# A gated MLP's second down projection: three pairs of weight-sum loads and ScalarE's transposing loads change places

## The chip, the cores and the metric

The kernel runs on one core of a Trainium2 chip. The metric is the device time of one execution in microseconds; the median of three runs counts. A profile of one execution shows what each engine did: PE (matrix multiply; PEld is its weight load), DVE (vector), ACT (scalar), POOL (GpSimd) and SP, which here only starts transfers. A q behind the name (SPq, ACTq) is the engine's queue of instructions that start transfers or wait.

## The reference

```python
x: (1, 2048, 1024) bf16;  w_gate, w_up: (1024, 3584);  w_down: (3584, 1024)
g = einsum("bsd,df->bsf", x, w_gate)
u = einsum("bsd,df->bsf", x, w_up)
h = gelu(g, tanh form) * u
out = einsum("bsf,fd->bsd", h, w_down)
```

## The kernel before

The 2048 rows of x are taken in two passes of 1024, each in two halves of 512 columns of the transposed x. A pass makes h (gate, up, gelu, product) and then runs its down projection. All large products are made with seven block products in place of eight, so sums and differences of blocks stand in for the blocks themselves; those of w_down are made once, in the first pass, written to a buffer in DRAM (`td`) and loaded again by each down projection. "Stored weight sums" are these.

The change is in the second down projection, `down(..., last=True)`, the last 103 us of the span (PE's first matmul of it starts at 436.82). It goes through numbered steps, mostly four or eight matmuls of 128x512 each. `step()` is called ahead of each group of matmuls and carries out what an agenda lists for that step: `at(last, step, what, ...)` fills it, from tables of step numbers. Within a step and between steps each engine's instructions stand in the order of the program text. The index j runs over 14 pairs of blocks of h and w_down.

- `load12(j)` loads the stored sums of pair j, two tiles q of 128x512 fp32 (L642; for some j as one larger tile m, L636, or w, L631). `LAST12[j]` is its step.
- `make12(j)` makes two sums of h on DVE (step `LAST12S[j]`).
- `fetch73(j)` loads raw blocks of w_down (L662, step `RAW73[j]`); `make73(j)`, step `LAST73[j]`, makes from them and from h three tiles on DVE and one cast on ACT (L677 for j under 8, L133 from 8).
- `apart`, steps 31 to 50, is one of the seven block products, itself split in the same way into products called K1, K2, K22, K3 and K4 (four steps each). Its results are split into 16-bit planes on ACT (L733) and written to DRAM by SP (`pt`, L734).
- `turn_back(quad, n)` loads these planes with a transposing transfer (L745): the eight of quad 0 from ACT's queue, the eight of quad 1 from SP's. `put_0` and `join_1` put them together on ACT (L750) and add them to what DVE stores; `put_0` also needs a tile of earlier sums (`ud`), loaded by SP at L757.

PE runs two loops. In the first one (steps 28 to 30 ahead of `apart`, 51 to 65 behind it) e(t) is four matmuls with the second tile of `load12(t)`, and c(t), which stands four steps later, four with the first; e(11) is the first to need a pair that the change moves. In the second one (steps 66 to 79) e(t) and c(t) use the tiles of `make73(t)`; c(6) to c(13) come last. Ahead of the second loop's e(0) ACT copies the four result banks of the first loop out (L138).

Every transfer ends by raising one of eight semaphores. The program deals these out in turn, in text order and over both queues together, and a transfer is not started until the previous one on its semaphore has landed. A queue starts its transfers in order, so a transfer that waits holds all those behind it.

Of the kernel before, what the change touches and what calls it, by code (L numbers as in the profile page):

```python
# [10 lines left out]
def kernel(  # L11
# [60 lines left out]
    D2 = 2 * P  # L72
    ORD4 = [*range(0, NJ, 2), *range(1, NJ, 2)]
    MSTEPS = 17
    LAST12 = [14, 15, 16, 29, 30, None, None, 41, 41, None, None, 49, 50, 51]
    LAST12S = [16, 18, 20, 34, 37, 40, 43, 45, 47, 49, 51, 53, 55, 57]
    BIG12L = (5, 9)
    RAW73 = [40, 40, 40, 40, 51, 51, 52, 53, 54, 55, 56, 57, 59, 59]
    LAST73 = [52, 53, 55, 57, 59, 61, 63, 65, 66, 68, 70, 71, 72, 73]
    LATE3 = 6  # L80

# [724 lines left out]
    def at(last, step, what, *args):  # L806
        agenda.setdefault((last, int(step)), []).append((what, args))

    for last in (False, True):
# [6 lines left out]
        for j in range(NJ):  # L816
            if (LAST12 if last else AT12)[j] is not None:
                at(last, (LAST12 if last else AT12)[j], load12, j, last)
            at(last, (LAST12S if last else AT12S)[j], make12, j, last)
            at(last, RAW73[j] if last else AT73[j] - 3, fetch73, j)  # L820
            at(last, (LAST73 if last else AT73)[j], make73, j, last)
# [7 lines left out]
    for i in range(NI):  # L829
        at(1, 2 * i, make_si, i)  # L830
    for n in range(2 * NS):
        at(1, 52 + n // 2, turn_back, 0, n)
        at(1, 63 + n, turn_back, 1, n)
    for i in range(NS):
        at(1, 69 + i, put_0, i)
# [488 lines left out]
```

## Time and profile before

| | us |
|---|---|
| median of 3 runs (541.85 to 543.47) | 542.02 |
| the profiled execution | 542.01 |
| its span, first to last instruction | 540.2 |
| PE busy in the span | 530.9 (98%) |
| DVE / ACT / POOL busy | 404.5 / 302.1 / 268.3 |
| mean granted TensorE clock | 0.994 |

The profiled execution is 1.8 us longer than its span; that part is taken as fixed. In the views below a line of the timeline gives the start, the length, the engine, the line of the program, the operation, tile written<-tiles read, shapes and the count, and in brackets the idle time before it with what ended it. Matmuls overlap, so a group's length is longer than its share: the next group's start tells the pace.

### The profile page before, as it was taken

How to read it: one execution, taken by the hardware profiler on the slowest of the kernel's cores; microseconds unless marked ns; L12 is line 12 of the kernel's file. 1: busy time of each engine (PE TensorE's matmuls, PEld its weight loads, DVE VectorE, ACT ScalarE, POOL GpSimd, SP SyncE). 2: the span in 40 equal slices, each digit the busy share in tenths (PEclk: the TensorE clock that was granted, in tenths of full speed). 3: DMA queues.
4: the chain of work that ended last, by engine and by line, in shares of the span. 5: the costliest groups of instructions: out<-in, count | busy, mean ns of one | idle time of the engine just before them, and what ended most of it. 6: DMA issues, size and time to landing. Idle time of an engine off the chain costs nothing.

```text
span 540.2 us, 7756 instructions
## 1 busy us (share of the span) xinstructions
PE 530.9 (98%) x2375; PEld 376.4 (70%) x2375; DVE 404.5 (75%) x645; ACT 302.1 (56%) x544; POOL 268.3 (50%) x259
## 2 busy tenths in 40 slices
PE   9999999999999999999999999999999999998797
PEld 5568686868686764688867586766866754776685
DVE  2989768787777786659699877657668598796875
ACT  3557686968686831016577775565666621371480
POOL 1079968979797950000005989796897500000000
PEclk9999999999999999999999999999999999999799
DMA  9795227685767799999997999928344798698943
GB/s 247 170 245 157 78 76 275 198 291 195 233 235 243 246 373 388 350 317 234 242 292 221 294 317 344 260 75 228 111 132 116 270 354 281 226 315 203 287 100 117
DMA packets 140729, 126.09 MB, mean 233 GB/s; under 512 B 31632, under 2 KB 119184, under 8 KB 140560
## 3 DMA queue, kind: packets, MB, share of 16 engines
q1 hardware_dynamic: 136336, 124.55, 75.4%
q10 hardware_dynamic: 4352, 1.05, 0.9%
q8 instruction: 19, 0.31, 0.2%
q14 instruction: 22, 0.18, 0.1%
HBM read 86.38 MB, written 31.06 MB: 217 GB/s over the span
## 4 chain that ended last, share of the span: by engine, by line
PE 93%; DMA 2%; DVE 2%; ACTq 1%; ACT 1%; issue 0%; SPq 0%; DVEq 0%
PE bank L145 92%; ACTq L745 1%; DMA q<-td 1%; DVE q L121 1%; PE bank L1057 1%; DMA w<-pt 1%; DVE xT L121 1%; PE bank L1002 1%; ACT s L875 0%; ACT xT L733 0%; ACT u L138 0%; DVE st L121 0%; ACT xT L677 0%; SPq L642 0%; ACTq L733 0%
## 5 line engine op out<-in xcount | busy, mean ns | idle before, releaser
L124 POOL TENSOR_TENSOR s<-w 128x512 fp32r<-128x512 bf16 x102 | 117.5, 1170 | 48.1 <-DMA w<-in_w_gate_dram 33.7
L145 PE MATMUL bank<-t,s 128*128 128x512 f32 x528 | 126.3, 392 | 0.0
L145 PEld LDWEIGHTS bank<-t,s 128*128 128x128 f32 x528 | 99.0, 188 | 21.6 <-POOL s L124 0.3
L145 PE MATMUL bank<-xT,w 128*128 128x512 bf16 (+1 forms) x504 | 110.2, 376 | 0.0
L145 PEld LDWEIGHTS <-w 128*128 128x128 bf16 x504 | 47.9, 98 | 57.9 <-issue 4.2
L213 ACT ACTIVATE g<-sum 128x512 f32<-128x512 f32 x81 | 51.5, 636 | 60.2 <-DVE sum L121 57.9
L138 ACT COPY p<-bank 128x512 f32<-128x512 f32 x98 | 55.1, 590 | 46.9 <-PE bank L145 46.8
L145 PE MATMUL bank<-q 128*128 128x512 f32 x224 | 57.5, 397 | 5.2 <-DMA q<-td 4.2
L121 DVE TENSOR_TENSOR hT<-g,bank 128x512 bf16<-128x512 f32 x72 | 49.0, 687 | 17.5 <-ACT g L213 12.1
L124 POOL TENSOR_TENSOR s<-w,s 128x512 fp32r<-128x512 bf16 x50 | 57.8, 1174 | 0.4
L124 POOL TENSOR_TENSOR s<-s,w 128x512 fp32r<-128x512 f32 x50 | 57.4, 1167 | 0.2
L121 DVE TENSOR_TENSOR bank<-bank,p 128x512 f32<-128x512 f32 x74 | 51.3, 695 | 5.9 <-PE bank L145 5.3
L145 PE MATMUL bank<-t,sa 128*128 128x512 f32 x216 | 54.9, 397 | 0.0
L145 PE MATMUL bank<-tb,s 128*128 128x512 f32 x216 | 54.3, 393 | 0.0
L199 POOL COPY seen<-t 128x1 f32<-128x1 f32 x2 | 0.4, 184 | 106.7 <-DVE t L121 106.7
L145 PEld LDWEIGHTS bank<-q 128*128 128x128 f32 x224 | 42.4, 190 | 15.6 <-DVE q L121 6.0
L145 PEld LDWEIGHTS bank<-t,sa 128*128 128x128 f32 x216 | 40.6, 188 | 9.1
L145 PEld LDWEIGHTS bank<-tb,s 128*128 128x128 f32 x216 | 40.5, 188 | 9.0 <-POOL s L124 0.3
L121 DVE TENSOR_TENSOR sum<-bank,p 128x512 f32<-128x512 f32 x54 | 37.0, 686 | 12.3 <-PE bank L145 11.3
L138 ACT COPY u<-bank 128x512 f32<-128x512 f32 x62 | 35.5, 596 | 17.5 <-PE bank L145 14.1
L133 ACT CAST tb<-raw 128x512 fp32r<-128x512 bf16 x20 | 12.5, 632 | 37.1 <-PE bank L145 24.2
L133 ACT CAST sa<-w 128x512 fp32r<-128x512 bf16 x54 | 30.7, 617 | 2.9 <-DMA out_dram<-st 2.9
(121 smaller groups left out, 736.8 us busy)
## 6 DMA issues: line engine op xcount, KB each, us to landing
raw<-in_w_down_dram SPq DMA_DIRECT2D x72, 256.0 KB, 5.5
w<-in_w_gate_dram SPq DMA_DIRECT2D x27, 512.0 KB, 4.5
w<-in_w_up_dram SPq DMA_DIRECT2D x27, 512.0 KB, 6.0
td<-m SPq DMA_DIRECT2D x11, 768.0 KB, 4.6
q<-td SPq DMA_DIRECT2D x28, 256.0 KB, 5.3
pd<-xT SPq DMA_DIRECT2D x10, 512.0 KB, 5.7
w<-td SPq DMA_DIRECT2D x5, 1024.0 KB, 7.8
p<-pd SPq DMA_DIRECT2D x20, 256.0 KB, 4.9
```

Source lines behind the costliest of these rows:

```text
L121: nc.vector.tensor_tensor(out=out, in0=a, in1=b, op=op)
L124: nc.gpsimd.tensor_tensor(out=out, in0=a, in1=b, op=op)
L133: nc.scalar.copy(out=t, in_=src)
L138: nc.scalar.copy(out=t, in_=ps)
L145: nc.tensor.matmul(ps, lhsT=lhs, rhs=rhs, start=start, stop=stop, skip_group_check=True)
L199: nc.gpsimd.tensor_copy(out=seen, in_=tile[:, :1].bitcast(f32))
L213: nc.scalar.activation(g, src, ACT.Gelu_apprx_tanh)
L745: queue.dma_start_transpose(out=turned["tp", quad][:, i, half], in_=pt[2 * quad + half][:, i * P : (i + 1) * P])
L1002: nc.tensor.transpose(tp[:, ko, :], xn[i][:, ko * P : (ko + 1) * P], ident)
L1057: nc.tensor.matmul(bank[3][:, :cols], lhsT=warm[:, :P], rhs=warm[:, :cols], start=True, stop=True)
```

## The change

Only step numbers change. `load12` of pairs 11, 12 and 13 moves from steps 49, 50, 51 to 40, 41, 49. `fetch73` of pairs 2 and 3 moves from step 40 to 48 and 49, and that of pair 4 from 51 to 50. The eight transposing loads of quad 0, which ACT starts, move from steps 52 to 55 to steps 56 to 59. No instruction is added or removed, and no size changes.

```diff
-    LAST12 = [14, 15, 16, 29, 30, None, None, 41, 41, None, None, 49, 50, 51]
+    LAST12 = [14, 15, 16, 29, 30, None, None, 41, 41, None, None, 40, 41, 49]
...
-    RAW73 = [40, 40, 40, 40, 51, 51, 52, 53, 54, 55, 56, 57, 59, 59]
+    RAW73 = [40, 40, 48, 49, 50, 51, 52, 53, 54, 55, 56, 57, 59, 59]
...
     for n in range(2 * NS):
-        at(1, 52 + n // 2, turn_back, 0, n)
+        at(1, 56 + n // 2, turn_back, 0, n)
         at(1, 63 + n, turn_back, 1, n)
```

In SP's order the two loads of pair 11 now stand behind the raw blocks of pairs 0 and 1, those of pair 12 behind the two m loads of pairs 7 and 8, those of pair 13 behind the first four plane writes; before, pairs 11 and 12 stood behind these four writes and pair 13 behind the last two writes and two raw loads. On ACT the first transposing load now stands behind the casts of pairs 0, 1 and 2; before, behind that of pair 0.

## The prediction

> **What bounds the kernel now.** I read the page's chain first, then the chain in order of time, then who waited for whom, then PE's timeline of the last stage, then that of the two queues.
>
> PE carries 93% of the chain, so only time in which PE waits, or runs slowly, can be won. The chain has one long piece that isn't PE's, and it ends in the load of a stored pair:
>
> ```profile
> 496.87 6.19 DMA q<-td
> 503.06 0.14 issue
> 503.19 33.69 PE bank L145 x136
> 536.88 0.02 issue
> 536.91 0.69 DVE st L121
> ```
>
> The waits (us in total, times, longest) name that load, a shorter wait of PE for DVE, and, of SP's queue, what held the loads:
>
> ```profile
> PE bank L145 <- DMA q<-td: 4.2, 1, 4.2
> PE bank L145 <- DVE q L121: 0.9, 1, 0.9
> SPq L642 <- DMA w<-pt: 4.6, 1, 4.6
> ```
>
> A stored-sum load (q) stood 4.6 us in SP's queue until a transposing load (w<-pt), started by ACT, had landed: the shared semaphores. PE's timeline shows the cost:
>
> ```profile
> 494.85 1.07 PE L145 MATMUL bank<-m,q 128*128 128x512 f32 x4
> 496.82 1.21 PE L145 MATMUL bank<-q 128*128 128x512 f32 x4 [0.90 <-DVE q L121]
> 497.87 1.09 PE L145 MATMUL bank<-m,q 128*128 128x512 f32 x4
> 503.19 2.05 PE L145 MATMUL bank<-q 128*128 128x512 f32 x4 [4.23 <-DMA q<-td]
> 505.04 3.36 PE L145 MATMUL bank<-w,q 128*128 128x512 f32 x8
> 508.23 6.53 PE L145 MATMUL bank<-q 128*128 128x512 f32 x28
> ```
>
> The matmul pace undisturbed is 0.2267 us (42 of them from 470.29 to 479.81). From 494.85 to the group at 514.61 stand 52 matmuls, 11.79 us at that pace; they took 19.76. So 7.97 us lie here: 1.06 ahead of e(12) at 496.82; 4.56 in the 8 matmuls up to e(13) at 503.19, nearly all idle; 2.32 in the 12 after it, which took 5.04 in place of 2.72; 0.03 in the rest. The 12 are slow because the granted clock fell, as the stretches (us, PE, PEld, DVE, ACT, POOL busy with counts, clock, DMA share, GB/s) show:
>
> ```profile
> 500.00:505.00 5.00, 1.81 (x4) 1.50 (x5) 3.58 (x6) 1.62 (x4) 0.00 (x0) 0.61 1.04 282
> 505.00:510.00 5.00, 5.00 (x17) 3.97 (x16) 4.06 (x7) 2.08 (x5) 0.00 (x0) 0.70 0.93 272
> ```
>
> And the queues, SP's loads and ACT's transposing loads:
>
> ```profile
> 480.61 10.62 SPq L642 DMA_DIRECT2D q<-td  x4
> 496.20 1.05 SPq L642 DMA_DIRECT2D q<-td  x2
> 484.57 4.59 ACTq L745 DMA_TRANSPOSE w<-pt  x2
> 489.21 5.30 ACTq L745 DMA_TRANSPOSE w<-pt  x4
> 494.58 2.60 ACTq L745 DMA_TRANSPOSE w<-pt  x2
> ```
>
> The four loads of pairs 11 and 12 took 10.62 us to start; the pair-13 loads at 496.20 landed at 503.06. ACT's eight starts kept its queue from 484.57 to 497.18, 12.61 us.
>
> **The stored pairs.** Six loads of 256 KB, started where four raw loads started before or close to it. Pair 11 starts at 466.9, where a raw load did (landing then: 472.07), and is needed at 493.95. Pair 12 stands behind the m loads: its first tile's slot is freed by DVE's add at 470.4, its second by K3's second matmul, at 474.1; two loads start at 470.5 and 474.1. Pair 13 starts behind the four plane writes, at about 482, needed at 497.6. None waits for a transposing load any more. So the 4.56 and the 2.32 go.
>
> **DVE's wait.** The 1.06 comes from DVE: its tile for raw pair 2 sat idle until 494.15, because the slot was one that a matmul on pair 6 still read. With the new order of allocations that tile's slot is freed by c(2)'s last matmul, which ends at 486.9. DVE then makes pair 2, the sums of pair 12, pair 3 and the sums of pair 13 without a stop at 0.605 us an operation (the pace at 501.10 to 502.30), provided the raw blocks are there. e(12) is due at 495.76 and needs sums that DVE finishes at about 492; e(13) is due at 497.57 and its sums end at about 495. The 1.06 goes too.
>
> **What the earlier loads delay.** Between the landings at 467.08 and 488.55, 6.5 MiB landed: 3.3 us per MiB, the transfers' engines busy throughout. Until the plane writes, two of the four raw loads give way and four q loads come in: 0.5 MiB more, 1.65 us. The w load of pairs 5 and 6 landed at 478.58, now 480.2, needed at 483.04; that of 9 and 10 at 485.22, now 486.9, needed at 490.32; the plane write whose buffer ACT reuses at 482.41 landed at 479.35, now 481.0. All stay covered, with 1.4 us the least. If the cover went, each us late is a us of PE. In SP's queue the w load now also stands behind the load that waits until 474.1: started at about 474.6 in place of 473.65, inside the same cover.
>
> **The raw blocks.** Raw pair 2 starts at about 480.6, where the first q load did (landing 487.26), so it lands at 488.9. DVE wants it at 489.4. Pairs 3 and 4 follow within some 3 us.
>
> **ACT's transposing loads.** The first one stands behind the cast of raw pair 2, so behind 488.9 in place of 484.57. The eight and their casts took 12.61 us, which brings the last start to 501.5. Behind them stand the four copies that free the banks for the second loop's e(0): one cast's step (0.52), then 0.48 apart and 0.59 long, done at 502.6, 503.1, 503.6, 504.1. Undisturbed, PE wants these banks at 503.01, 503.24, 503.46, 503.69, so the last one costs 0.4 us. Of the 12.61, the first start alone is 3.28; it could be 1.28 like the others, and this wait is then nothing; or, if it lasts until the transfers already queued have landed (some 1.75 MiB here, to about 494), 5.2, and the wait is 2.3. I take the 3.28 of the only row of its kind.
>
> **SP's transposing loads and the adds behind them.** SP's last raw load waits for the semaphore of ACT's last transposing load. That starts at 500.2; the last two took 4.65 and 6.14 to land, the median of eight was 3.9. With 4.65 it is 504.9; then 0.4 for the raw load and 1.2 for SP's first transposing load, and the `ud` load starts at 506.5 (508.43 before) and lands 5.21 later, 511.7. DVE needs it for its first stored add, and behind that stand 15 operations in order, 9.1 us, up to the tile for e(13): 520.8. e(13) at the undisturbed pace is due at 520.49: 0.3. With 6.14 it is 1.8, with 3.9 nothing. This wait and ACT's lie on one path, so the larger counts, not the sum. The end is as before: PE's last 32 matmuls, one add, one store.
>
> **The sum.** 542.01 - 7.97 + 0.4 = 534.4, the profiled execution against itself; it stands at the median, so 534.4 is also the forecast of the median. Bounds: 534.0 with no wait left, 536.3 with the late start of ACT's loads.
>
> [...]
>
> **The rivals.** *ACT's queue is late* (535.0 to 536.9, chance 0.22): the 5.2 or the 6.14 above, or a raw pair 2 that lands at 490. For it: ACT's first start did take 3.28, and the last one 6.14 to land. Against: ACT's seven others took 1.27 to 1.36 beside running loads.
>
> [...]
>
> *The moved loads crowd the others* (537 to 540, chance 0.05): the w load of pairs 5 and 6 lands after 483.04 and PE waits there. The slowest landing of this stage, 9.31 us for a tile started at 442.78, would bring it to 483.9 and cost 0.8; for more, several loads must be that slow at once.
>
> *Nothing is won* (within 0.3%, chance 0.03): pair 13 or DVE's tile would still wait. Against: the order of starts and the slots.
>
> *Slower: ACT's starts take twice their time* (about 547, chance 0.07). Everything that frees e(0)'s banks stands behind the eight starts. At 217.26 a transposing load of SP's took 2.93 us to start, and at 24.57 one took 5.26, both with much in flight. At 2.97 each the eight take 23.8 us, to 512.7; e(0) starts at about 513.9, 2.9 us later than before, and some 2.3 more go to the slow clock behind an idle PE. It decides from 20.6 us for the eight, or from a raw pair 2 that lands after 496.9. Against: before, seven of eight took 1.3 in the same traffic.
>
> **How the numbers follow.** The forecast itself (533.7 to 535.0) has 0.60. A measurement of this kernel tells about 0.3%, 1.6 us, from no change. Faster holds the forecast, late ACT, clock and crowding: 0.60 + 0.22 + 0.03 + 0.05 = 0.90; same 0.03; slower 0.07. The range 533.4 to 536.9 holds the forecast and late ACT, 0.82; its low end leaves room for the spread of the runs.
>
> **What would show it.** PE's timeline after: one unbroken pace from 483 to 503, no idle time put down to q<-td or to DVE ahead of e(12) and e(13), the clock at 1.00 in 500:510, and the second loop starting at about 503.4. ACT's transposing loads from about 489 to 501.5. SP's L642 never waiting for w<-pt. DVE's first stored add at about 511.7. Wrong would be a wait of PE ahead of 484 (crowding), a wait for ACT's bank copies of over 2 us (late ACT), or a group of slow matmuls with the clock at 0.5.

## The result, and the profile after

The changed kernel takes 534.95 us in the median of 4 runs (534.14 to 536.67), against 542.30 for the kernel before beside it: a ratio of 0.9865, with a 95% interval of 0.9836 to 0.9895. A second set of runs gave 534.90 and 0.9857 (0.9837 to 0.9876). The profiled execution took 535.19, its span 533.4 (540.2 before). The forecast was 534.4, in a range of 533.4 to 536.9. One run of the kernel with SP's transposing loads later, further down, took 595.75 us at a mean clock of 0.851, and the ratio there leaves that run out.

The end of the chain in order of time (start, length, what carried it) shows no load of a stored pair any more. What stands in its place is the `ud` load and DVE's operations behind it:

```profile
482.73 24.14 PE bank L145 x106
506.87 5.35 DMA w<-ud
...
520.23 1.22 DVE q L121 x2
521.49 8.53 PE bank L145 x36
530.05 0.69 DVE st L121
```

PE's timeline, where before stood 4.23 us of waiting and a group of slow matmuls:

```profile
497.61 1.07 PE L145 MATMUL bank<-q 128*128 128x512 f32 x4
498.52 1.98 PE L145 MATMUL bank<-w,q 128*128 128x512 f32 x8
500.33 6.51 PE L145 MATMUL bank<-q 128*128 128x512 f32 x28
...
521.49 1.20 PE L145 MATMUL bank<-q 128*128 128x512 f32 x4 [0.79 <-DVE q L121]
```

The first line is e(13). From the group ahead of e(12) at 494.89 to the second loop's c(0) at 506.68 the 52 matmuls take 11.79 us, where they took 19.76. (The second loop's e(0) to e(3) are the last 16 of the 28 at 500.33.) The last line is the second loop's e(13): the only wait left. The clock stays up, where it stood at 0.70 (us, PE, PEld, DVE, ACT, POOL busy with counts, clock, DMA share, GB/s):

```profile
505.00:510.00 5.00, 5.00 (x24) 4.06 (x23) 1.22 (x3) 5.00 (x7) 0.00 (x0) 1.00 0.55 157
```

The waits of SP's queue (us in total, times, longest) no longer hold a line that says L642 waited for w<-pt. The wait for transposing loads has moved to the raw loads. PE does not wait for these, but the last of them holds the `ud` load behind it:

```profile
SPq L662 <- DMA w<-pt: 8.5, 5, 2.7
SPq L642 <- PE bank L145: 4.8, 5, 3.3
```

And ACT's queue:

```profile
488.87 2.57 ACTq L745 DMA_TRANSPOSE w<-pt  x2
491.50 5.21 ACTq L745 DMA_TRANSPOSE w<-pt  x4
496.78 2.58 ACTq L745 DMA_TRANSPOSE w<-pt  x2
```

The eight starts run from 488.87 to 499.36, 10.5 us.

One thing in the kernel's description has to be put right here: the semaphores are dealt in turn over both queues, but not in the order of the text. In the kernel before, ACT's first two transposing loads (step 52) have the two semaphores ahead of those of pair 11's loads (step 49): by its trace 103 and 104 of the eight, which are 101 to 108, and those loads 105 and 106. Each queue keeps the order of the text. So moving a step of ACT's also changes which of SP's loads inherits a transposing load's semaphore: in the changed kernel ACT's first two have 105 and 106.

### The profile page after: what moved, and what is told of

Same layout as the page of the kernel before. It is cut to its first block, busy times and chain, and to the rows that moved or that the text cites. A ratio compares the mean times of both kernels' runs of the same rounds, so it can differ in the third digit from the quotient of the medians.

```text
span 533.4 us, 7753 instructions
## 1 busy us (share of the span) xinstructions
PE 528.2 (99%) x2375; PEld 374.2 (70%) x2375; DVE 404.2 (76%) x645; ACT 301.9 (57%) x544; POOL 268.3 (50%) x259
## 4 chain that ended last, share of the span: by engine, by line
PE 94%; DVE 3%; DMA 2%; SPq 0%; issue 0%; DVEq 0%
PE bank L145 94%; DVE q L121 2%; DMA w<-ud 1%; DMA xn<-in_x_dram 1%; DVE xT L121 1%; DVE st L121 0%; SPq L995 0%; PE bank L1002 0%; DVEq L121 0%
```

## The experiments

Theory A: two causes made the 7.97 us, the semaphore that held pair 13's loads behind a transposing load, and the slot that DVE's tile for raw pair 2 waited for. Rival B: the transposing loads' traffic made the load slow, so only their move counts. Rival C: the earlier loads are all that counts. The three edits were undone one by one and two by two.

**The loads alone.**

```diff
-    LAST12 = [... 49, 50, 51]
+    LAST12 = [... 40, 41, 49]
```

> Only the six loads of pairs 11 to 13 move (steps 40, 41, 49); the raw loads and ACT's transposing loads stay. Theory A (two separate causes: DVE's tile for raw pair 2 waits for a slot, and the loads of pair 13 stand behind a transposing load's semaphore): the second cause goes, the first stays, so the wait for q<-td (4.2) and the low clock go, PE still waits about 1 us for DVE ahead of e(12), and again about as much ahead of e(13), since DVE then makes the sums of pair 13 late as well: 536.4 to 537.3. Rival B (the traffic of the transposing loads itself makes the load slow): as these loads start where they did, PE still waits some us: 540 to 542. Rival C (the earlier loads are all that counts): as the changed kernel, 534.5 to 535.5.

Measured: 540.41 (539.28 to 540.69), ratio 0.9956 (0.9942 to 0.9971). The time is the one that B gave, the waits are not: pair 13's load was in time, and A and C missed. PE's timeline:

```profile
485.74 1.19 PE L145 MATMUL bank<-w,q 128*128 128x512 f32 x4 [1.97 <-DMA w<-td]
...
499.03 1.20 PE L145 MATMUL bank<-q 128*128 128x512 f32 x4 [0.30 <-DVE q L121]
...
502.24 1.20 PE L145 MATMUL bank<-q 128*128 128x512 f32 x4 [1.09 <-DVE q L121]
```

The last two lines are A's: the load's wait is gone and DVE's stands ahead of e(12) and of e(13). The first line is the prediction's rival of crowding, which the changed kernel does not show. Four raw loads still stand ahead, and raw tiles and q tiles come from one ring of slots. So the second load of pair 11 waited in SP's queue for a slot until 474.75, and two m loads, pair 12 and the w load of pairs 5 and 6 stood behind it: that w load started at 477.04 (474.58 in the changed kernel) and landed at 485.70, where PE wanted it at 483.6.

**The transposing loads alone.**

```diff
-        at(1, 52 + n // 2, turn_back, 0, n)
+        at(1, 56 + n // 2, turn_back, 0, n)
```

> Only ACT's eight transposing loads move (steps 56 to 59); SP's order is that of before. Theory A: the loads of pair 13 are still dealt a semaphore behind a transposing load (now the fourth), so the wait for q<-td stays, and DVE's wait for its tile too: 539.5 to 542.5, with a wait of 3 to 5 us for q<-td. Rival B (traffic): the load of pair 13 has less beside it and lands in time, only DVE's 1 us and what follows stay: 535 to 537.

Measured: 538.66 (536.78 to 542.30, 12 runs), ratio 0.9932 (0.9909 to 0.9954): less than A expected, more than B. PE's timeline:

```profile
497.36 1.21 PE L145 MATMUL bank<-q 128*128 128x512 f32 x4 [0.90 <-DVE q L121]
...
501.00 1.17 PE L145 MATMUL bank<-q 128*128 128x512 f32 x4 [1.51 <-DMA q<-td]
```

Pair 13's loads started at 495.98 and 496.41, as before (496.20 and 496.87), since SP's queue was still held: its plane writes waited 4.0 us for w<-pt, its q loads 0.6. But the later one landed in 4.45 us and not in 6.19. So B may have a part. In both kernels two transposing loads and two raw loads were still under way when it started, but here the transposing ones had started 2.5 and 3.8 us ahead of it, before 1.0 and 2.3, and a plane write was under way as well. The start is A's; that the 1.7 us of the landing are traffic fits, but which transfer made them no run separates. The wide spread of the runs is told at the end.

**The loads and the raw blocks** (transposing loads left at 52 to 55).

> Loads and raw blocks move as in the changed kernel, ACT's transposing loads stay at steps 52 to 55. Theory A: both causes are gone without the move of the transposing loads; the first of these waits for the semaphore of the last K4 plane write, so it starts at about 488 anyway: 534.3 to 535.5, no wait for q<-td, none for DVE ahead of e(12). Rival B (traffic, the four steps are needed): a wait of 3 us or more for q<-td and 538 or more.

Measured: 535.54 (534.21 to 536.23), ratio 0.9863 (0.9845 to 0.9881): the changed kernel, without its third edit. ACT's first transposing load stood behind the landing of the fourth plane write (K3's second, where K4's last was expected) and started at 489.67 (488.87 in the changed kernel). No wait for q<-td, and none for DVE ahead of e(12). The profiled execution (536.23) has the changed kernel's last wait, 1.21 us at the second loop's e(13). B falls as an account of the change.

**The raw blocks alone.**

```diff
-    RAW73 = [40, 40, 40, 40, 51, ...]
+    RAW73 = [40, 40, 48, 49, 50, ...]
```

> Only the raw blocks move (pairs 2 and 3 to steps 48 and 49, pair 4 to 50); the loads of pairs 11 to 13 and ACT's transposing loads stay. Theory A: DVE's tile slot comes free in time, so no wait for DVE ahead of e(12); the loads of pair 13 stand behind the landing of the first and second transposing loads, so they start at about 492 to 494 and land at 495 to 500, and PE waits 0 to 2.5 us for q<-td: 534.5 to 538. Rival C (the earlier loads are all that counts): only the 1 us of DVE is won, the wait for q<-td stays at 4: 540.5 to 541.5.

Measured: 536.25 (535.26 to 537.05), ratio 0.9877 (0.9860 to 0.9894). C falls: with pairs 11 to 13 where they stood, most of the gain is there. DVE's wait is gone, and pair 13's loads started at 494.71 and 495.85, behind the landings of the first two transposing loads; PE waited 1.25 us for the second, with the clock at 1.00:

```profile
499.82 1.16 PE L145 MATMUL bank<-q 128*128 128x512 f32 x4 [1.25 <-DMA q<-td]
```

That load started 1.0 us sooner than before (496.87) and landed in 3.83 us.

**The raw blocks and the transposing loads** (loads back at 49, 50, 51).

> The changed kernel with the six stored-sum loads of pairs 11 to 13 back at steps 49, 50, 51. The pair-13 loads are then dealt semaphores of a pair-12 load and of a plane write, neither of a transposing load. Theory A (a load is late only as far as the semaphore ahead of it is): the two loads start at about 492 and 494.5 and land by 498.5, and PE waits 0 to 1 us for q<-td ahead of e(13) due at about 497.7: 534.5 to 536.3, between the changed kernel and the one with the raw blocks alone (536.25), and no wait of SP for w<-pt ahead of a stored-sum load. Rival C (the earlier steps of the loads are what counts): the wait for q<-td is 3 us or more, 538 to 541.

Measured: 534.78 (534.39 to 535.04), ratio 0.9852 (0.9834 to 0.9869): the changed kernel's time, without the edit after which the change is named. Pair 13's loads started at 492.26 and 493.56, landed at 496.69 and 497.81, and e(13) went off at 498.06 with no wait.

**The loads and the transposing loads** (raw blocks back at 40).

> The changed kernel with the raw blocks back at step 40 for pairs 2 and 3 (pair 4 at 51). If the four raw loads ahead of the w load of pairs 5 and 6 are what made PE wait 2.0 us for it in the kernel with the loads alone, that wait is here again, with DVE's two waits of 0.3 and 1.1: 539.5 to 541. If that wait came from where ACT's transposing loads stood, it is gone: 536.5 to 538.

Measured: 540.02 (539.23 to 540.56), ratio 0.9948 (0.9932 to 0.9963), with the same three waits as the loads alone (1.93 for w<-td, 0.30 and 1.10 for DVE). The crowding comes from the raw loads that stay ahead.

With these the table is full. Each ratio is against the kernel before on the same chip:

| moved | ratio | us won |
|---|---|---|
| loads | 0.9956 | 2.3 |
| transposing loads | 0.9932 | 4.1 |
| raw blocks | 0.9877 | 6.5 |
| loads, transposing loads | 0.9948 | 2.6 |
| loads, raw blocks | 0.9863 | 7.2 |
| raw blocks, transposing loads | 0.9852 | 7.8 |
| all three | 0.9857 | 7.7 |

**Pair 13's loads alone, one step earlier**, to see the first cause without the crowding:

```diff
-    LAST12 = [... 49, 50, 51]
+    LAST12 = [... 49, 50, 50]
```

> The kernel before with one number changed: the two loads of pair 13 at step 50 in place of 51, so in SP's order they stand right behind pair 12's, ahead of the last two plane writes and two raw loads. This takes the crowding (which the six loads moved together brought) out of the first cause. Theory A: the loads start at about 491.5 and 494.6 (the second behind the landing of the fourth transposing load) in place of 496.2 and 496.9 and land by 499, so the wait for q<-td is under 0.5 us and the clock stays at 1.00; DVE's wait ahead of e(12) stays (0.9), and DVE's sums of pair 13 are late for e(13) by about 1 us: 536.0 to 537.2. If the whole 7.97 hangs on pair 13's load alone: 534.5 to 535.3. If the load is slow for the traffic beside it, and not for its start: 539 or more.

Measured: 536.83 (536.64 to 537.14), ratio 0.9883 (0.9868 to 0.9898), the time that A gave. One number, moved by one step, won 6.4 us:

```profile
497.27 1.20 PE L145 MATMUL bank<-q 128*128 128x512 f32 x4 [0.30 <-DVE q L121]
...
500.48 1.20 PE L145 MATMUL bank<-q 128*128 128x512 f32 x4 [1.09 <-DVE q L121]
```

No wait for q<-td, and DVE's wait in both places (ahead of e(12) 0.30, where 0.9 was expected). The moved loads came a little later than expected: the load ahead of them waited for a transposing load until 491.84, so the pair 13 loads started at 492.21 and 495.80 and landed at 496.23 and 499.41. SP's stored-sum loads waited 7.4 us for w<-pt here, more than the 4.6 before. So waiting for a transposing load is not in itself what cost the time; it is how late the load then started and landed.

**The `ud` load earlier**, on top of the change, against its one remaining wait:

```diff
-    at(1, 63, fetch_u3)
+    at(1, 58, fetch_u3)
```

> The changed kernel with the load of the ud tile at step 58 in place of 63: it now stands ahead of the last two raw pairs and of SP's transposing loads, and no longer behind the landing of ACT's last transposing load. If that landing (7.14 us in place of the 4.65 of the sum) is what made the last wait, the ud tile lands by 505, the wait of DVE's first stored add and the 0.8 us of PE ahead of the second loop's e(13) go, and the time is 0.8 to 1.1 us under the changed kernel's: 533.5 to 534.3. If the wait comes from DVE's own queue of work instead, PE still waits there and the time is that of the changed kernel, 534.7 to 535.5.

Measured: 534.77 (533.95 to 538.62), ratio 0.9862 (0.9837 to 0.9887): no difference from the change, and neither reason was the right one. The load was started 7 us sooner, but landed only at 509.47 (9.74 us). DVE (first fence) began its stored adds 2.8 us sooner and then lost it; SP's queue (second fence) says why:

```profile
509.56 0.69 DVE L121 TENSOR_TENSOR st<-gt,w 128x512 bf16<-128x512 f32 x1 [2.93 <-DMA w<-ud]
519.77 0.69 DVE L121 TENSOR_TENSOR st<-gt,w 128x512 bf16<-128x512 f32 x1 [2.90 <-DMA out_dram<-st]
```

```profile
507.18 10.44 SPq L745 DMA_TRANSPOSE w<-pt  x7
517.73 0.52 SPq L850 DMA_DIRECT2D out_dram<-st  x1
```

The fourth stored add needs a tile whose output store stands behind seven of SP's transposing starts, 10.44 us. A wait removed was replaced by the next one, and PE again waited 0.79 us for DVE at the second loop's e(13).

**SP's transposing loads later** (66 to 73 in place of 63 to 70), first without and then with the earlier `ud` load:

```diff
-        at(1, 63 + n, turn_back, 1, n)
+        at(1, 66 + n, turn_back, 1, n)
```

> The changed kernel with SP's eight transposing loads at steps 66 to 73 in place of 63 to 70. In SP's order the ud load now stands ahead of all eight, and each of the four output stores that follow DVE's stored adds stands ahead of the transposing loads of its step. Expected if what held the kernel with the ud load moved alone was the output store behind seven transposing starts (9 us): the ud load starts at about 505.7 and lands at about 511, DVE's first stored add 1.2 us sooner than in the changed kernel, no wait of DVE for out_dram<-st, and no wait of PE ahead of the second loop's e(13): 533.7 to 534.5, at most 1 us under the changed kernel. Against: the transposing loads themselves end later (about 519 in place of 517) and could hold the last adds: then 535 to 537.

> Both: the ud load at step 58 and SP's transposing loads at steps 66 to 73. The ud tile lands by about 509.5, the output stores no longer stand behind seven transposing loads, so DVE's adds run through and PE has no wait in the second loop: 533.5 to 534.4, with no wait of DVE for out_dram<-st. If a wait of PE for DVE of 0.8 us is still there, the cause was neither.

Measured: 534.92 for the first (ratio 0.9845, 0.9831 to 0.9858; the `ud` tile at 511.96, not 511, because raw pair 2 landed at 489.42 and ACT's last transposing load landed at 506.50; so the second loop's last 20 matmuls of e still took 5.13 us and not 4.71), and 534.27 (534.04 to 534.48), ratio 0.9837 (0.9824 to 0.9851), for both together. In the latter DVE's stored adds begin at 506.70, DVE doesn't wait for out_dram<-st, and the chain is PE alone to the end:

```profile
482.67 46.23 PE bank L145 x201
...
528.92 0.69 DVE st L121
```

This is the fastest version, with a spread of 0.4 us in its runs; the 0.6 us to the changed kernel lie within the two intervals.

**The changed kernel once more.**

> The changed kernel itself, run beside the next three so that they can be compared on one chip. Expected: 534.5 to 535.5, the landing of ACT's last transposing load 6.5 to 7.5 us after its start, and a wait of 0.5 to 1.3 us for DVE ahead of the second loop's e(13).

Measured: 534.90 (534.37 to 536.03). Its profiled execution (534.37) had no wait at the second loop's e(13), where 0.5 to 1.3 us were expected: raw pair 2 landed at 487.57 and not at 488.78, so ACT's last transposing load landed at 503.64 and not at 505.21. The remaining wait comes and goes with one landing.

## Why the prediction was right, point by point

*The stored pairs.* Held. The loads of pair 12 started at 470.53 and 474.21 (said: 470.5 and 474.1), pair 13's at 481.89 and 482.79 (about 482), none behind a transposing load. The 4.56 and the 2.32 went: 52 matmuls in 11.79. But the attribution was too simple. The 4.6 us in SP's queue were a wait of pair 12's second load (started at 490.90); pair 13's stood behind it in the queue, and behind a plane write (until 494.65) and a raw load (until 495.69) that waited for transposing loads too. The wait needed two things, the late start and a landing of 6 us; with the raw blocks moved, 1.25 us of it were left, and either of the other two edits took those. Why moving the raw blocks shortened the landing to 3.83 us no run separates.

*DVE's wait.* Held: the tile was free in time and DVE ran without a stop from 482.59 to 506.2. The slot was worth more than the 1.06 given to it: it made pair 13's sums late too, which the load had hidden (0.30 idle ahead of e(12) and 1.09 ahead of e(13) when only pair 13 moved).

*What the earlier loads delay.* The cover held, thinner than said. The w load of pairs 5 and 6 landed at 481.33 (480.2), 1.7 us before its matmuls began; the plane write at 482.01 (481.0), just ahead of ACT's copy at 482.16; the w load of pairs 9 and 10 at 486.73 (486.9). The rival of crowding is real where the raw loads stay: 2 us. The transfers' engines, called busy throughout, were busy for 0.92 of the stretch that gave the 3.3 us per MiB (467.08 to 488.55). The price of crowding was read from the wrong row: the slowest landing of the stage before was not 9.31 but 9.57 us, of the tile started at 439.12, which makes it 1.1 and not 0.8.

*ACT's transposing loads.* Start right (488.87 for 488.9), length wrong: 10.5 and not 12.61, as the first start took 1.25 and not 3.28. The bank copies were done at 502.0 (said: 504.1) and the second loop's e(0) went off at about 503.05, so their 0.4 was nothing. In the runs the first start took 3.25 to 3.64 us in every kernel with the raw blocks of pairs 2 and 3 at step 40, and 1.23 to 1.59 in every one with them moved. Why is not shown, but the 3.28 belonged to an order that the change gave up.

*SP's transposing loads and the adds.* Here lies the mis-sized term. The last transposing load started 2.1 us earlier than said but took 7.14 to land and not 4.65; the two errors nearly cancelled (505.21 for 504.9). With the `ud` load 5.35 long and not 5.21, the first add came at 512.32 (511.7), and e(13) at 521.49 against 520.53 due: 0.96 where 0.3 stood. The nearer row was there: of the two landings quoted, 6.14 was that of this same last transfer, and in the runs it took 5.24 to 7.81, but for one with 3.39. With the start as predicted, though, it would have given 1.8, about as far off on the other side. That the total came so close is in part luck: the 0.4 in it stood for ACT's wait, which did not come, and the wait that came was the other one. The sum with what was measured: PE 0.04 later ahead of the stretch, 7.97 won in it, 1.07 lost in the second loop, so 542.01 + 0.04 - 7.97 + 1.07 = 535.15; the execution took 535.19.

*The slow clock.* The 2.32 us counted from the rows held: three executions in which PE waited 0.1 us at most took 534.04, 534.37 and 534.69; the sum without a wait said 534.0. They differ mostly by when PE came to this stretch (the group at 483.04 before starts at 483.01, 483.36 and 483.53). The chances give 0.03 to the clock, a slow stretch that costs more than the rows count; no run shows that. In the kernel before, 2.05 us of the slow stretch lay in the wait, which the sum counts in its 4.56 (see the end).

*The slower rival* did not come: ACT's eight starts took 1.25 to 1.28 each. Nor did the late start of ACT's loads; by the prediction's own 3.3 us per MiB its 1.75 MiB would have been 5.8 and not 5.2 us.

## What to carry to other kernels

When a load is late, ask first what it was queued behind, not how long it took: here a semaphore shared with another queue's transposing load (4.6 us of SP's queue), a slot of a shared ring (4.63 us of DVE, up to 494.15), and then an output store behind seven transposing starts (10.44 us) each held work that had nothing to do with them. Gains of edits that cure the same wait did not add (2.3, 4.1 and 6.5 alone, 7.7 together), and the edit that names a change need not be the one that does the work: try them apart. For a transfer's landing take the row of that same transfer before that of a neighbour, and look at what will be queued in front of it then: a row of the old order need not hold in the new one (ACT's first start took 3.28 us, then 1.25).

## What the runs showed of the hardware

The two falls of the clock seen here lasted 6.84 and 3.42 us, and of two waits of about 2 us only one was followed by a fall. Stretches of 1 us of the kernel before, and of the one with the loads and the transposing loads moved (columns as above):

```profile
501.00:502.00 1.00, 0.00 (x0) 0.00 (x0) 1.00 (x3) 0.02 (x1) 0.00 (x0) 0.57 0.84 244
507.00:508.00 1.00, 1.00 (x3) 0.74 (x3) 0.78 (x2) 0.08 (x1) 0.00 (x0) 0.51 1.06 342
```

```profile
486.00:487.00 1.00, 1.00 (x4) 0.75 (x3) 1.00 (x2) 0.73 (x1) 0.00 (x0) 0.58 1.04 425
489.00:490.00 1.00, 1.00 (x5) 0.83 (x4) 0.96 (x2) 0.95 (x2) 0.00 (x0) 0.71 1.04 375
```

The stretches between stood at 0.50, those on either side at 1.00. The second fall came behind this wait:

```profile
485.24 1.31 PE L145 MATMUL bank<-w,q 128*128 128x512 f32 x4 [1.93 <-DMA w<-td]
```

If the clock stood at one of these two values all the time, 0.57 puts the fall at 501.14 and 0.51 the return at 507.98: 6.84 us. In the second kernel it is 486.16 to 489.58: 3.42, half as long, and it began 0.9 us after PE had started again, so the matmuls paid for nearly all of it (eight took 3.34 in place of 1.81). It came behind a wait of 1.93 us; one of 1.97 in the same place, with the loads alone, left the clock at 1.00 in its profiled execution. In the kernel before, the clock fell 2.2 us after PE had stopped (498.96 to 501.14). What sets the moment and the length of a fall was not shown.

So after a wait of about 2 us PE ran on at full speed in one execution and lost 1.5 us more in another; what decided it, no run shows. In the six runs of that second kernel the four with a mean clock of 0.996 or 0.997 took 539.99 to 540.56, the two with 0.999 or 1.000 539.23 and 539.61. The runs with the transposing loads alone fall in two groups as well: the five with a mean clock of 0.993 to 0.997 took 539.54 to 542.30, the seven with 0.999 or 1.000 took 536.78 to 539.25. That the clock is the cause there, and not a sign of a longer wait, was not shown run by run. In the kernel before, 2.05 of the 6.84 us lay in the wait itself; at 0.50, half of the other 4.79 is lost, an estimate of 2.40 against the 2.32 counted.
